# Linear attention and a highway layer: PSUM shared in four slots, weights cast by 128-row blocks, and a new order list

## The chip, the core and the metric

The kernel runs on one core of a Trainium2 chip. Its engines are TensorE (PE; PEld is its weight loading), VectorE (DVE), ScalarE (ACT), GpSimd (POOL) and SyncE (SP, which here only issues DMAs). PE writes its results to PSUM, eight banks of 128 x 512 fp32; DVE and ACT read and write PSUM, POOL does not in this kernel. The metric is the time of one execution on the device in microseconds, median over runs.

## What is computed

For 8 batches, 8 heads, 576 rows and head size 64, all fp32:

```python
q_s = softmax(q, axis=-1);  k_s = softmax(k, axis=2)      # over features; over rows
kv  = einsum('bhsd,bhse->bhde', k_s, v)                   # 64 x 64 per head
x   = einsum('bhsd,bhde->bhse', q_s, kv)  -> [4608, 512]
H = max(x @ w_h, 0);  T = sigmoid(x @ w_t + b_t)
out = T * H + (1 - T) * x
```

With th = tanh(z / 2) the gate is (1 + th) / 2. The kernel halves w_h - I on casting it, so that d = max(x(w_h - I)/2, -x/2) and out = (1 + th) * d + x.

## The kernel before

The 4608 rows are 36 tiles of 128. Batches go in pairs: tiles 9p to 9p+3 belong to the first, 9p+4 to 9p+7 to the second, 9p+8 to both. A step is named by its kind, a tile or batch, and a part; a suffix names its engine (A, D, P) or a variant.

Per batch: `k_`, `v_`, `q_` are loads on SP's queue (landing buffers for three batches); `ek` and `eq` are exponentials on ACT (`:F` for all of a batch in one); `vc` casts v to fp16 (POOL, unless A or D); `kv` is 72 small matmuls into a pair of banks, with the sums of k in an extra column; `kr`, `kn` (DVE) normalise it to fp16. `qt` transposes exp(q) on PE, `qc` copies that to SBUF.

Per tile: `xu` (PE, a pair of banks), `rs` and `x` (DVE) give normalised x; `xt` transposes it on PE and `xe` copies it to SBUF (ACT, or DVE with D); `mh` and `mt` are four 512-column matmuls each against w_h and w_t. `bw` seeds `mt`'s bank with the bias: a copy of `ball` on ACT or DVE, or, without a suffix, a matmul on PE. `th` is the tanh, `dd` gives d, `uu` gives (1 + th) * d on DVE from PSUM, or with `:P` in two instructions on POOL (L578, L579); `oo` adds x on POOL, `st` stores. Tiles 0, 4 and 5 (`HALVED`) go in two halves of heads, and the last tile, 35, in two halves of columns. `fill_n` are n matmuls of zeros.

`ORDER` (L16) is a list written out by a search; the program issues the steps in its sequence, so it fixes the sequence on each engine and on SP's queue, while across engines only data and buffers make one wait. An engine never passes a waiting step, and SP never passes a waiting DMA.

PSUM before: `ps_t` gives two banks in turn to the `mt` results, `ps_g` two to the `mh` results and the halved `xu`. The other four banks are two slots (`space`, L183), each either one pair or two singles; `kv`, `xu`, `qt` and `xt` use them. A transpose with `:W` takes one bank and 128-row matmuls; without it, it takes a pair and twice as many matmuls of 64 rows. A seed by ACT or DVE is added to by matmuls with `start=False`.

Weights before: each of four landed pieces of w_h and w_t (two 128-row blocks, 128 x 1024) is cast in one instruction, `whc` (L275) and `wtc` (L264); `whd` subtracts the identity first, block by block, on POOL.

## Time and profile before

| what | us |
|---|---|
| median of 3 runs | 119.06 |
| lowest and highest | 118.78, 119.47 |
| the profiled execution's own time | 118.52 |
| its span, first to last instruction | 116.7 |
| mean granted TensorE clock | 0.988 |

The profile shows one execution. Busy time is given per engine; a row of a timeline or of a group has start or count, duration, engine, source line, the operation, and the tiles written and read. Idle time before a row is put down to what ended it. The chain of waits is followed back from the last instruction. Loading takes 30.41 MB from HBM, storing 9.44 MB.

### The profile page before, as it was taken

How to read it: one execution, taken by the hardware profiler on the slowest of the kernel's cores; microseconds unless marked ns; L12 is line 12 of the kernel's file. 1: busy time of each engine (PE TensorE's matmuls, PEld its weight loads, DVE VectorE, ACT ScalarE, POOL GpSimd, SP SyncE). 2: the span in 40 equal slices, each digit the busy share in tenths (PEclk: the TensorE clock that was granted, in tenths of full speed). 3: DMA queues.
4: the chain of work that ended last, by engine and by line, in shares of the span. 5: the costliest groups of instructions: out<-in, count | busy, mean ns of one | idle time of the engine just before them, and what ended most of it. 6: DMA issues, size and time to landing. Idle time of an engine off the chain costs nothing.

```text
span 116.7 us, 3816 instructions
## 1 busy us (share of the span) xinstructions
PE 107.1 (92%) x1544; PEld 57.3 (49%) x1544; DVE 92.4 (79%) x216; ACT 90.7 (78%) x132; POOL 90.0 (77%) x104
## 2 busy tenths in 40 slices
...
GB/s 46 376 401 377 409 397 386 376 375 389 391 390 389 389 392 360 376 386 371 371 359 395 385 405 387 378 383 371 404 389 187 275 386 237 274 190 359 340 288 176
DMA packets 24198, 40.62 MB, mean 348 GB/s; under 512 B 5363, under 2 KB 11763, under 8 KB 24181
## 3 DMA queue, kind: packets, MB, share of 16 engines
...
q8 instruction: 12, 0.20, 0.7%
...
HBM read 30.41 MB, written 9.44 MB: 341 GB/s over the span
## 4 chain that ended last, share of the span: by engine, by line
PE 70%; DMA 14%; POOL 5%; issue 3%; DVE 2%; SPq 1%; ACT 1%; DVEq 0%; POOLq 0%
PE tps L539 25%; PE gps L547 24%; DMA w32t<-in_moe_w_t_dram 9%; DMA v<-in_v_dram 5%; PE pair L449 4%; PE one L504 4%; PE pair L316 4%; PE one L402 3%; POOL v L306 2%; PE pair L496 2%; PE pair L376 1%; POOL u L579 1%; POOL o L599 1%; DVE u L581 1%; PE pair L458 1%
## 5 line engine op out<-in xcount | busy, mean ns | idle before, releaser
L599 POOL TENSOR_TENSOR o<-u,x 128x512 f32<-128x512 f16 (+1 forms) x36 | 40.5, 1141 | 3.0 <-DVE u L581 2.0
L539 PE MATMUL tps<-w16t,xT 128*128 128x512 f16 (+1 forms) x144 | 36.6, 377 | 0.3 <-DVE tps L527 0.3
L547 PE MATMUL gps<-w16h,xT 128*128 128x512 f16 x144 | 36.8, 380 | 0.0
L567 DVE SCALAR_TENSOR_TENSOR d<-x,gps 128x512 f16<-128x512 f16 x36 | 24.2, 675 | 0.2 <-PE gps L547 0.2
L579 POOL TENSOR_TENSOR u<-g,d 128x512 f16<-128x512 f16 x19 | 21.9, 1155 | 2.7 <-DVE d L567 1.3
L306 POOL CAST v<-v 128x1152 f16<-128x1152 f32 (+1 forms) x13 | 12.3, 958 | 11.0 <-DMA v<-in_v_dram 11.0
L480 DVE TENSOR_TENSOR x<-pair,rs 128x512 f16<-128x512 f32 x27 | 18.2, 685 | 1.2 <-POOL o L599 0.2
L539 PEld LDWEIGHTS <-xT 128*128 128x128 f16 x148 | 12.9, 98 | 12.2 <-DVE xT L515 0.7
L300 ACT ACTIVATE ek<-k 128x576 f16<-128x576 f32 (+2 forms) x15 | 17.9, 1222 | 1.2 <-DMA k<-in_k_dram 1.2
L547 PEld LDWEIGHTS <-xT 128*128 128x128 f16 x144 | 12.5, 98 | 11.9 <-ACT xT L515 0.3
L525 ACT COPY tps<-ball 128x512 f32<-128x512 f32 x22 | 13.1, 594 | 3.8 <-DVE u L581 3.6
L561 ACT ACTIVATE th<-tps 128x512 f16<-128x512 f32 x19 | 11.3, 593 | 2.6 <-PE tps L539 2.5
L214 PE MATMUL one<-blank 128*128 128x512 f16 x40 | 11.4, 429 | 1.5 <-POOL blank L145 1.3
L578 POOL TENSOR_SCALAR g<-th 128x512 f16<-128x512 f16 x19 | 11.7, 617 | 0.7 <-ACT th L561 0.7
L581 DVE SCALAR_TENSOR_TENSOR u<-tps,d 128x512 f16<-128x512 f32 (+1 forms) x17 | 11.4, 670 | 1.0 <-ACT tps L563 0.5
L358 ACT ACTIVATE qe<-q 128x1024 f16<-128x1024 f32 (+3 forms) x9 | 9.2, 1052 | 3.3 <-DMA q<-in_q_dram 3.3
L563 ACT ACTIVATE tps<-tps 128x512 f32<-128x512 f32 (+1 forms) x17 | 9.8, 575 | 1.8 <-PE tps L539 1.8
L504 PE MATMUL one<-idh,x 128*128 128x128 f16 x100 | 9.5, 219 | 1.4 <-DVE xT L515 1.0
L504 PEld LDWEIGHTS <-x 128*128 128x128 f16 x100 | 7.1, 98 | 6.2 <-DVE x L485 1.4
L515 ACT COPY xT<-one 128x512 f16<-128x512 f16 (+1 forms) x13 | 6.9, 532 | 2.3 <-PE one L504 1.6
L353 ACT ACTIVATE qe<-q 128x1024 f16<-128x1024 f32 (+1 forms) x7 | 8.0, 1175 | 0.0
L449 PEld LDWEIGHTS <-eq 64*128 64x128 f16 (+1 forms) x240 | 4.6, 97 | 6.4 <-issue 5.5
...
## 6 DMA issues: line engine op xcount, KB each, us to landing
k<-in_k_dram SPq DMA_DIRECT2D x6, 1152.0 KB, 12.4
v<-in_v_dram SPq DMA_DIRECT2D x6, 1152.0 KB, 12.4
...
q<-in_q_dram SPq DMA_DIRECT2D x2, 1152.0 KB, 13.0
...
```

The lines of the kernel that those rows point to most:

```text
L300: nc.scalar.activation(t[:, :, c:c + n].rearrange("p j c d -> p c j d"), T[f"k32{b}"][:, c:c + n].rearrange("p c (j d) -> p c j d", j=NJ), ...
L306: copy(v16[b % NV][:, c:c + n, :, 0:D], T[f"v32{b}"][:, c:c + n].rearrange("p c (j d) -> p c j d", j=NJ))
L480: nc.vector.tensor_mul(t.rearrange("p k (w h) e -> p w k h e", w=2), pairs(i)[:, :, :, 1:129].rearrange("p w k (h e) -> p w k h e", h=2), ...
L504: nc.tensor.matmul(t[:, n], T[f"x{i}"][:, n0 + n % 2:n0 + 2 * P:2], idh, is_transpose=True, start=True, stop=True, skip_group_check=True)
L525: nc.scalar.copy(t[:, cs], ball[:, cs])
L539: nc.tensor.matmul(T[gate(i, k)][:, cs], T[f"xT{i}"][:, n], w16["t"][:, n, cs], start=False, stop=(n == parts[-1] and not first), skip_gro ...
L547: nc.tensor.matmul(t, T[f"xT{i}"][:, n], w16["h"][:, n], start=(first and n == parts[0]), stop=(n == parts[-1] and not (first and len(part ...
L567: nc.vector.scalar_tensor_tensor(t, T[f"x{i}"], -0.5, T[f"gps{i}"], op0=ALU.mult, op1=ALU.max)
L578: nc.gpsimd.tensor_scalar(g, T[f"th{i}"], 1.0, 1.0, op0=ALU.add, op1=ALU.mult)
L579: nc.gpsimd.tensor_mul(t, g, T[f"d{i}"])
L581: nc.vector.scalar_tensor_tensor(t[:, cs], T[gate(i, h)][:, cs], 1.0, T[f"d{i}"][:, cs], op0=ALU.add, op1=ALU.mult)
L599: eng.tensor_add(t[:, cs], T[f"u{i}_{h}"][:, cs], T[f"x{i}"][:, cs])
```

## The change

All eight banks are now four slots of two banks, and every step that uses PSUM asks for space in them. `bank_users` names the user of each step and what it wants: a pair, a single, a single written over its whole width by matmuls (full), or a single that ACT or DVE seeds, which must have been full or seeded before. `grant` walks the list once, when the program is built, and gives each user banks whose last user stands earlier in the list; a slot changes its form when both its banks are free. Pairs prefer slots 2 and 3 (banks 4 to 7). Weights are cast in eight instructions of 128 x 512, `whb` and `wtb`, one per 128-row block. The list is searched anew: loads, stores, engines and tile order differ from the 41st step on. By count: fills 40 matmuls to 33; `bw` on PE 6 to 5, on ACT 22 to 24, on DVE 9 to 8; `uu` on POOL 19 to 20; `xe` on DVE 19 to 27; `qc` on ACT 7 to 9; `vc` on POOL 13 to 11, on DVE 1 to 4; `qt` with `:W` 9 to 7.

```diff
 ORDER = """
 b_0 q_0_0 v_0_1 setupdve k_0_0 b_32 eq_0_0 bsplit setuppool fill_5 fill_8 bp v_0_0 bc qt_0_0 ek_0_1 v_0_3 ek_0_0 k_0_2
 v_0_2 vc_0_3:A bw_1 vc_0_0 ek_0_2 vc_0_2 q_0_4 vc_0_1:D ek_0_3 bw_0 w_h_0 fill_8 qc_0_0 whd_1:P kv_0_0 eq_0_1 w_h_2
-w_t_2 kr_0_0 whd_0:P whd_2:P setuplate w_t_0 k_1_2 v_1_2 q_1_0 k_1_0 v_1_0 fill_5 q_1_4 kn_0_0 q_2_0 k_2_0 eq_0_2
-xu_0_0 v_2_0 q_3_0 rs_0_0 whc_0:A x_0_0 k_3_0 fill_4 v_3_0 kv_0_1 fill_3 kr_0_1 kn_0_1 xu_0_1 rs_0_1 xu_1_0 rs_1_0
-qt_0_1 x_1_0 fill_6 whd_3:P qc_0_1 xt_1_0 xu_3_0 qt_0_2 qc_0_2:A xe_1_0:D fill_1 rs_3_0 x_3_0 x_0_1 xt_3_0 xu_2_0
-rs_2_0 whc_2:A x_2_0 xe_3_0 mh_1_0 mh_3_0 wtc_2 xt_2_0 dd_1 wtc_0:P mt_1_0 th_1_0 ek_1_2 xe_2_0:D xt_0_0 vc_1_3 xt_0_1
-ek_1_3 bw_3:D mh_2_0 mt_3_0 dd_2 xe_0_1:D xe_0_0 vc_1_2 eq_1_0 uu_1_0:P oo_1_0 th_3_0 ek_1_1 mt_0_1 kv_1_1 qt_1_0
-ek_1_0 dd_3 kr_1_1 kn_1_1 vc_1_0 mh_0_1 mh_0_0 mt_0_0 qc_1_0 xu_5_1 bw_2 rs_5_1 vc_1_1:A kv_1_0 th_0_0 bw_5:A mt_2_0
-eq_1_2 x_5_1 xt_5_1 dd_0 eq_1_1 qt_1_2 kr_1_0 kn_1_0 qc_1_2 xu_5_0 rs_5_0 x_5_0 xu_4_0 xe_5_1 xu_8_0 q_4_0 qt_1_1
-th_2_0 rs_8_0 xt_5_0 x_8_0 xe_5_0:D uu_3_0:P qc_1_1:A rs_4_0 mt_5_1 x_4_0 oo_3_0 mh_5_1 mt_5_0 bw_8:A xt_8_0 xe_8_0:D
-th_5_0 xu_6_0 xu_4_1 mh_5_0 uu_0_0:P oo_0_0 mt_8_0 uu_2_0:P eq_2_1 rs_6_0 x_6_0 xt_6_0 eq_2_0 th_8_0 rs_4_1 dd_5
-xu_7_0 mh_8_0 rs_7_0 uu_5_0:P qt_2_0 xe_6_0:D x_4_1 mh_6_0 x_7_0 ek_2_0:F xt_4_1 qc_2_0 qt_2_1 dd_8 qc_2_1 vc_2_2
-xe_4_1:D xt_4_0 bw_6 xe_4_0 mt_6_0 uu_8_0 bw_4:D qt_2_2 mh_4_0 vc_2_0:A xt_7_0 kv_2_0 oo_5_0 qc_2_2:A dd_6 mh_4_1
...
-qc_7_2:A xt_34_0 bw_30:A qc_6_2:A st_17_0 uu_31_0:P st_32_0 th_33_0 st_23_0 xu_35_0 st_14_1 dd_33 rs_35_0 uu_33_0
-xe_34_0 bw_34:A oo_33_0 x_35_0 dd_30 mt_30_0 st_16_1 th_30_0 uu_30_0 mh_34_0 xt_35_0:W mt_34_0 st_33_0 xe_35_0 oo_31_0
-th_34_0 mh_35_0 oo_30_0 bw_35_0 st_31_0 mt_35_0 st_30_0 bw_35_1 mt_35_1 th_35_0 dd_34 uu_34_0 oo_34_0 st_34_0 dd_35
-uu_35_0 oo_35_0 st_35_0 th_35_1 uu_35_1 oo_35_1:D st_35_1:A
+w_t_2 kr_0_0 whd_0:P whd_2:P w_t_0 kn_0_0 whb_0 fill_8 k_1_2 kv_0_1 k_1_0 whd_3:P kr_0_1 xu_0_0 kn_0_1 xu_0_1 qt_0_1
+wtb_3:P eq_0_2 rs_0_0 wtb_0:P x_0_0 q_1_4 whb_2 rs_0_1 fill_4 qc_0_1 x_0_1 xt_0_0 xe_0_0:D xt_0_1 xe_0_1:D v_1_2
+xu_3_0 v_1_0 rs_3_0 whb_3:D x_3_0 mh_0_1 xt_3_0 whb_1:D mh_0_0 dd_0 wtb_2 wtb_1:P q_1_0 mt_0_1 xu_1_0 q_2_0 setuplate
+rs_1_0 x_1_0 xe_3_0 qt_0_2 qc_0_2 ek_1_2 ek_1_3 mh_3_0 dd_3 bw_3 mt_3_0 xt_1_0 th_3_0 ek_1_1 v_2_0 xu_2_0 mt_0_0
+th_0_0 xe_1_0:D uu_0_0:P vc_1_3 vc_1_2 mh_1_0 eq_1_2 rs_2_0 x_2_0 xt_2_0 xe_2_0:D bw_6:D mt_1_0 eq_1_1 dd_1 uu_3_0
+bw_8:A bw_2:A mh_2_0 qt_1_1 vc_1_1 ek_1_0 qc_1_1:A dd_2 k_2_0 kv_1_1 vc_1_0:D kv_1_0 kr_1_1 qt_1_2 qc_1_2:A kn_1_1
+q_3_0 eq_1_0 th_1_0 mt_2_0 kr_1_0 th_2_0 kn_1_0 xu_6_0 qt_1_0 rs_6_0 x_6_0 eq_2_0 qc_1_0 xt_6_0 xe_6_0:D xu_8_0 rs_8_0
+xu_5_0 oo_0_0 eq_2_1 rs_5_0 x_8_0 mt_6_0 xu_5_1 xu_4_0 oo_3_0 xt_8_0 x_5_0 uu_1_0:P uu_2_0:P mh_6_0 k_3_0 rs_4_0
+rs_5_1 xu_4_1 th_6_0 xe_8_0:D xt_5_0 mt_8_0 vc_2_2 x_5_1 xt_5_1 qt_2_1 rs_4_1 xe_5_0:D x_4_1 xe_5_1:D x_4_0 dd_6
+th_8_0 mh_8_0 uu_6_0 mh_5_1 bw_5:A xt_4_0 qc_2_1:A vc_2_0 xt_4_1 xe_4_0:D xu_7_0 mt_5_0 v_3_0 bw_4:A rs_7_0 ek_2_0:F
+dd_8 oo_2_0 qt_2_0 mh_5_0 xe_4_1:D qc_2_0 x_7_0 mh_4_0 mt_5_1 dd_5 uu_8_0:P mh_4_1 oo_8_0 qt_2_2 qc_2_2 xt_7_0
+xe_7_0:D kv_2_0 bw_7:A kr_2_0 th_5_0 q_4_0 eq_3_0:F oo_6_0 kn_2_0 mt_7_0 th_7_0 dd_4 xu_11_0 rs_11_0 xu_10_0 rs_10_0
+x_10_0 x_11_0 mt_4_0 mh_7_0 uu_5_0:P xt_10_0:W xu_12_0 dd_7 xe_10_0 xt_11_0 xe_11_0:D bw_10:A mt_4_1 mh_10_0 th_4_0
+ek_3_2 rs_12_0 uu_7_0 oo_1_0 x_12_0 mt_10_0 uu_4_0 xt_12_0:W xe_12_0:D oo_5_0 ek_3_0 xu_9_0 rs_9_0 v_4_0 vc_3_0 qt_3_1
+x_9_0 mh_11_0 vc_3_2 qc_3_1 mh_12_0 xt_9_0:W th_10_0 dd_10 bw_12:A qt_3_0:W qt_3_2:W k_4_0 dd_11 kv_3_0 oo_4_0 qc_3_2
+mt_12_0 xe_9_0 q_5_0 qc_3_0:A kr_3_0 kn_3_0 dd_12 xu_17_0 bw_9:A bw_11:D xu_14_0 oo_7_0 eq_4_0:F uu_10_0:P rs_14_0
+x_14_0 th_12_0 oo_10_0 bw_14:A mh_9_0 mt_9_0 xt_14_0:W rs_17_0 uu_12_0:P mt_11_0 dd_9 xe_14_0:D mh_14_0 th_9_0 x_17_0
+uu_9_0 xu_13_0 qt_4_0 vc_4_2:A th_11_0 xt_17_0:W mt_14_0 rs_13_0 x_13_0 xu_16_0 qc_4_0:A xe_17_0:D bw_17:A dd_14
+xu_15_0 mh_17_0 mt_17_0 xt_13_0:W ek_4_0:F rs_15_0 oo_12_0 oo_9_0 rs_16_0 vc_4_0 x_15_0 th_17_0 uu_11_0:P dd_17
+th_14_0 xt_15_0:W oo_11_0 x_16_0 qt_4_1 bw_13:A kv_4_0 xe_13_0:D mh_13_0 xe_15_0:D v_5_0 uu_17_0 oo_17_0 bw_15:A
+kr_4_0 eq_5_0 qc_4_1 kn_4_0 xt_16_0:W vc_5_2:D q_4_9 xe_16_0:D mt_13_0 xu_20_0 xu_19_0 rs_19_0 v_6_0 rs_20_0 mt_15_0
+mh_15_0 dd_13 uu_14_0:P oo_14_0 mh_16_0 x_19_0 eq_5_1 xt_19_0 th_13_0 x_20_0 vc_5_0:A q_5_9 qt_5_1 dd_15 qc_5_1
+bw_16:A mt_16_0 xu_18_0 st_5_0 eq_5_2 k_5_0 th_15_0 uu_15_0 st_1_0 xe_19_0 qt_5_0 xt_20_0:W dd_16 mh_19_0 th_16_0
+xe_20_0:D bw_20:A mh_20_0 rs_18_0 x_18_0 dd_19 qc_5_0:A uu_13_0:P xu_21_0 xt_18_0 ek_5_0:F bw_19:D mt_20_0 mt_19_0
+qt_5_2:W st_1_1 eq_4_2 q_6_0 xe_18_0:D mh_18_0 th_19_0 st_3_1 oo_13_0 th_20_0 rs_21_0 x_21_0 bw_18:A qt_4_2:W dd_20
+st_14_1 uu_19_0 kv_5_0 dd_18 qc_4_2:A qc_5_2:A xt_21_0:W kr_5_0 kn_5_0 eq_6_1 mt_18_0 bw_21:A eq_6_0 xu_23_0 xe_21_0:D
+rs_23_0 xu_26_0 rs_26_0 mh_21_0 mt_21_0 uu_16_0:P oo_15_0 x_26_0 oo_16_0 x_23_0 th_18_0 xt_26_0:W xe_26_0 qt_6_0
+xt_23_0 dd_21 qt_6_1:W st_3_0 bw_23:D xe_23_0:D qc_6_0 st_14_0 mh_26_0 vc_6_0 xu_24_0 xu_22_0 uu_20_0:P oo_20_0
+th_21_0 bw_26:A mt_23_0 dd_26 st_5_1 oo_19_0 rs_24_0 vc_6_2:A rs_22_0 mh_23_0 x_24_0 x_22_0 mt_26_0 k_6_0 ek_6_0:F
+th_23_0 xt_24_0 kv_6_0 uu_18_0:P dd_23 qc_6_1 xe_24_0:D uu_23_0 th_26_0 kr_6_0 q_7_0 st_10_1 kn_6_0 v_7_0 xt_22_0:W
+uu_21_0:P mh_24_0 k_7_0 xe_22_0:D oo_21_0 oo_18_0 oo_23_0 xu_25_0 xu_28_0 rs_25_0 st_12_0 st_10_0 bw_24:A bw_22:A
+mt_24_0 mt_22_0 q_6_9 rs_28_0 x_25_0 xu_29_0 x_28_0 xt_25_0 dd_24 q_7_9 eq_7_0 qd_7_0 eq_7_1 qd_7_1 rs_29_0 xt_28_0:W
+th_24_0 mh_22_0 x_29_0 xe_25_0 th_22_0 xe_28_0:D xu_30_0 xt_29_0 uu_26_0:P rs_30_0 xe_29_0 oo_26_0 mh_28_0 mh_29_0
+dd_22 uu_22_0:P mh_25_0 st_19_0 uu_24_0:P bw_25:D dd_28 ek_7_0:F x_30_0 vc_7_2:A xu_27_0 bw_28:D rs_27_0 oo_22_0
+vc_7_0:D xt_30_0 mt_25_0 mt_28_0 xe_30_0 kv_7_0 dd_25 dd_29 th_25_0 oo_24_0 kr_7_0 mh_30_0 st_21_0 th_28_0 st_7_0
+uu_28_0 bw_30:A mt_30_0 st_17_0 uu_25_0:P x_27_0 xt_27_0 kn_7_0 xu_31_0 bw_29:A mt_29_0 st_12_1 bw_27:D xe_27_0:D
+mt_27_0 rs_31_0 x_31_0 xt_31_0 dd_30 bw_31:D eq_7_2 th_29_0 st_8_0 xu_34_0 rs_34_0 th_30_0 mh_27_0 st_16_0 xe_31_0
+oo_25_0 st_25_0 x_34_0 st_7_1 qt_7_2:W qc_7_2 mt_31_0 st_23_0 xt_34_0 dd_27 st_26_0 xu_33_0 eq_6_2 uu_29_0:P mh_31_0
+rs_33_0 th_27_0 bw_34:A xe_34_0:D qt_6_2:W qc_6_2:A th_31_0 mt_34_0 oo_29_0 x_33_0 xu_35_0 dd_31 oo_28_0 xu_32_0
+uu_27_0 rs_32_0 xt_33_0:W mh_34_0 uu_31_0 xe_33_0 bw_33:A th_34_0 x_32_0 mh_33_0 xt_32_0:W uu_30_0:P oo_30_0 st_30_0
+oo_31_0 st_31_0 dd_34 rs_35_0 uu_34_0 xe_32_0 mt_33_0 oo_34_0 oo_27_0 bw_32:A x_35_0 st_34_0 mh_32_0 th_33_0 xt_35_0:W
+xe_35_0 dd_33 uu_33_0 st_16_1 mt_32_0 th_32_0 st_28_0 oo_33_0 dd_32 uu_32_0 oo_32_0 st_33_0 mh_35_0 bw_35_0 bw_35_1
+mt_35_0 st_32_0 th_35_0 dd_35 mt_35_1 th_35_1 uu_35_0 oo_35_0 uu_35_1 st_35_0 oo_35_1:D st_35_1:A
...
     PS = bass.MemoryType.PSUM
-    ps_t = pool("ps_t", 2, space=PS)
-    ps_g = pool("ps_g", 2, space=PS)
...
+    def bank_users(step):
...
+        if kind in ("xu", "rs", "x"):
+            return [(f"xu{at[0]}_{at[1]}", "single" if at[0] in HALVED else "pair")]
+        if kind in ("kv", "kr", "kn"):
+            return [(f"kv{at[0]}", "pair")]
...
+        if kind == "bw" and at[0] < LAST:
+            return [(gate(at[0], 0), "seeded" if e else "full")]
...
+        if kind in ("mh", "dd"):
+            return [(f"gps{at[0]}", "full")]
...
+    place, held, shape, whole = {}, [None] * 8, ["single"] * 4, [False] * 8
+    SPARE = 0
+    def grant(user, want, now):
+        last = [-1 if h is None else final[h] for h in held]
+        free = [n < now for n in last]
+        idle = [free[2 * k] and free[2 * k + 1] for k in range(4)]
+        form = "pair" if want == "pair" else "single"
+        may = lambda k: shape[k] == form or (idle[k] and (k >= 2 or idle[k + 2]))
+        if want in ("pair", "early"):
+            k = min((k for k in (3, 2, 1, 0) if idle[k] and may(k)),
+                    key=lambda k: (want == "early" and k != 3, k < 2, max(last[2 * k:2 * k + 2])))
+            mine = [2 * k, 2 * k + 1]
+        else:
+            mine = [min((n for n in range(8) if free[n] and may(n // 2)), key=lambda n: (
+                want == "seeded" and not whole[n],
+                (3 if shape[n // 2] == "pair" else 2 if n >= 4 and free[n ^ 1] else 0) + (SPARE * (want == "single" and whole[n])),
+                last[n]))]
+            assert want != "seeded" or whole[mine[0]]
+        for n in mine:
+            held[n], whole[n] = user, want in ("seeded", "full")
+        shape[mine[0] // 2] = form
+        place[user] = (mine[0] // 2, form, mine[0] % 2)
...
     def space(user, n=None):
+        k, want, one = place[user]
+        if form[k] != want:
+            reopen(k, want)
+        return rooms[k][one if n is None else n]
...
+    def wt_cast(e, n):
+        src, dst = T[f"wt{n // 2 * 2}"][:, n % 2], w16["t"][:, n]
+        if e == "D":
+            nc.vector.tensor_scalar_mul(dst, src, 1.0)
+        else:
+            (nc.gpsimd.tensor_copy if e == "P" else nc.scalar.copy)(dst, src)
...
     def bw(e, i, h=0):
-        if i < LAST or h == 0:
-            t = T[gate(i, h)] = ps_t.tile([P, DM], FP32, tag="tps", name=f"tps_{i}_{h}")
-        else:
-            t = T[gate(i, h)] = space("last")[:, 0]
+        t = T[gate(i, h)] = space(gate(i, h))
...
     def mh(e, i, k):
-        t = once(f"gps{i}", lambda: ps_g.tile([P, DM], FP32, tag="gps", name=f"gps_{i}"))
+        t = once(f"gps{i}", lambda: space(f"gps{i}"))
```

120 lines of the change are left out of this document (44 added, 76 removed).

## The prediction

> **What bounds the kernel now.** I read the page first (busy time, then the chain of waits), then the windows, the chain in order of time, and last the timelines of the start and the end.
>
> ```profile
> span 116.7 us, 3816 instructions
> ...
> PE 107.1 (92%) x1544; PEld 57.3 (49%) x1544; DVE 92.4 (79%) x216; ACT 90.7 (78%) x132; POOL 90.0 (77%) x104
> ...
> GB/s 46 376 401 377 409 397 386 376 375 389 391 390 389 389 392 360 376 386 371 371 359 395 385 405 387 378 383 371 404 389 187 275 386 237 274 190 359 340 288 176
> ...
> PE 70%; DMA 14%; POOL 5%; issue 3%; DVE 2%; SPq 1%; ACT 1%; DVEq 0%; POOLq 0%
> ```
> ```profile
> 24.00:28.00 4.00, 3.39 (x65) 2.00 (x58) 2.91 (x9) 3.77 (x8) 3.66 (x5) 1.00 1.07 380
> ...
> 40.00:112.00 72.00, 71.46 (x1158) 37.75 (x1143) 64.27 (x138) 61.78 (x92) 66.27 (x66) 1.00 0.99 347
> ```
>
> The columns of a window are its length, then the busy time of PE, PEld, DVE, ACT and POOL, the granted clock, the DMA share and GB/s. From 40 to 112 us PE is busy in 71.46 of 72.00 us, and 70% of the chain is PE: this stretch ends when PE's work ends. POOL (66.27) and DVE (64.27) are close behind. The DMA engines are full too (share 0.99): 359 to 409 GB/s in slices 2 to 30 of 40, on average 385.
>
> The start is set by arrivals. Here an entry in brackets is the idle time before an instruction and what ended it.
>
> ```profile
> 7.88 10.72 DMA w32t<-in_moe_w_t_dram
> ...
> 39.80 0.81 PE pair L316 x67
> ...
> 64.89 0.39 issue
> ...
> 69.87 0.45 PE one L397 x8
> ...
> 82.46 0.62 PE pair L316 x71
> ...
> 88.24 0.37 PE pair L376 x16
> ...
> 102.37 0.86 PE gps L547 x4
> ```
> ```profile
> 17.78 1.89 PE L547 MATMUL gps<-w16h,xT 128*128 128x512 f16 x8
> ...
> 26.20 0.66 POOL L306 CAST v<-v 128x576 f16<-128x576 f32 x1 [0.18 <-DMA v<-in_v_dram]
> ...
> 37.41 1.14 POOL L306 CAST v<-v 128x1152 f16<-128x1152 f32 x1 [0.78 <-DMA v<-in_v_dram]
> ...
> 34.68 2.11 ACT L300 ACTIVATE ek<-k 128x2304 f16<-128x2304 f32 x1
> ...
> 37.68 0.27 PE L504 MATMUL one<-idh,x 128*128 128x128 f16 x2 [0.98 <-DVE xT L515]
> ```
>
> The last weight lands at 18.6, the last piece of v of batch 1 at 26.2, v of batch 2 at 37.4. PE waits for the last time at length (0.98) before 37.68; from `kv_2_0` at 39.80 to its last matmul it runs on, with 0.39 us of gap.
>
> ```profile
> 111.25 0.60 PE L539 MATMUL pair<-w16t,xT 128*128 128x256 f16 x4
> ...
> 38.51 3.38 POOL L599 TENSOR_TENSOR o<-u,x 128x512 f32<-128x512 f16 x3
> ...
> 107.91 5.28 POOL L599 TENSOR_TENSOR o<-u,x 128x512 f32<-128x512 f16 x5 [0.72 <-DVE u L581]
> ...
> 112.82 0.42 DVE L599 TENSOR_TENSOR o<-pair,x 128x256 f32<-128x256 f32 x1
> ```
>
> PE ends at 111.85, POOL at 113.19, DVE at 113.24; then the last stores. So POOL ends level with DVE's last add. The 38.51 row begins with `oo_5_0`, the first POOL step behind `kv_2_0` in the list; an add is 3.38 / 3 = 1.13.
>
> **The change part by part.** The prices used:
>
> ```profile
> L581 DVE SCALAR_TENSOR_TENSOR u<-tps,d 128x512 f16<-128x512 f32 (+1 forms) x17 | 11.4, 670 | 1.0 <-ACT tps L563 0.5
> L413 DVE COPY eq<-one 128x1024 f16<-128x1024 f16 x8 | 5.5, 688 | 0.7 <-PE one L402 0.3
> L515 DVE COPY xT<-one 128x512 f16<-128x512 f16 x12 | 4.9, 416 | 1.9 <-PE one L504 1.9
> L515 DVE COPY xT<-one 128x256 f16<-128x256 f16 x3 | 0.8, 281 | 0.0
> L515 ACT COPY xT<-one 128x512 f16<-128x512 f16 x10 | 5.8, 583 | 0.6 <-PE one L504 0.4
> L485 DVE TENSOR_TENSOR x<-pair,rs 128x512 f16<-128x512 f32 x6 | 4.1, 690 | 0.2
> L485 DVE TENSOR_TENSOR x<-xu,rs 128x256 f16<-128x256 f32 x6 | 2.5, 422 | 0.2
> L473 DVE RECIPROCAL rs<-pair 128x8 f32<-128x8 f32 x6 | 1.2, 204 | 0.6 <-PE pair L458 0.4
> L279 ACT ACTIVATE w16h<-w32h 128x1024 f16<-128x1024 f32 x2 | 2.1, 1058 | 0.9 <-POOL w32h L273 0.9
> L269 POOL CAST w16t<-w32t 128x1024 f16<-128x1024 f32 x1 | 1.0, 1037 | 2.4 <-DMA w32t<-in_moe_w_t_dram 2.4
> L306 DVE CAST v<-v 128x576 f16<-128x576 f32 x1 | 0.8, 754 | 0.0
> L283 DVE CAST b<-b 1x512 f16<-1x512 f32 x2 | 0.8, 384 | 1.3 <-DMA b<-in_moe_b_t_dram 1.3
> ACT tps L525 <- DVE u L581: 3.6, 6, 0.8
> 57.90 0.61 POOL L578 TENSOR_SCALAR g<-th 128x512 f16<-128x512 f16 x1
> 58.60 1.16 POOL L579 TENSOR_TENSOR u<-g,d 128x512 f16<-128x512 f16 x1
> 59.84 1.16 POOL L599 TENSOR_TENSOR o<-u,x 128x512 f32<-128x512 f16 x1
> k<-in_k_dram SPq DMA_DIRECT2D x6, 1152.0 KB, 12.4
> ```
>
> *Banks.* What the fixed rings of two cost is ACT's seed copies waiting for DVE's `uu` (3.6 us in total, 0.8 at most); PE has no row for a bank. Following `grant` down the new list, every pair goes to slots 2 and 3 (banks 4 to 7) and all but eleven single users after the start go to banks 0 to 3: much as before. I price the sharing itself at nothing; between -0.98 (PE's one long wait goes) and +0.8 (one such bank wait moves onto PE).
>
> *Weights.* Four casts of 128x1024 become eight of 128x512: ACT 3, POOL 3, DVE 2. ACT gains 3 x 0.5 us, POOL pays three halves of 1.04 for one whole (+0.5), DVE pays 2 x 0.384 to 2 x 0.754; I take 0.69 each, near the wide row, since all 128 partitions are cast. Behind `whb_0` on ACT waits `eq_0_2`; behind `whb_3` and `whb_1` on DVE wait `x_3_0` and `dd_0`. All of it is hidden: batch 0 is through PE before v of batch 1 (26.2) lets `kv_1_0` start. Without that cover the three POOL and DVE pieces would cost up to 1.5 us.
>
> *Fills and biases.* 40 fill matmuls become 33, seven of 0.216 (0.86 / 4), before 18 us where PE waits for arrivals: nothing on the path. One bias matmul less, also early.
>
> *Batch 1.* The loads of batch 1 arrive in another order; q_1_4 (640 KB) instead of q_1_0 (512) lies before `v_1_0`, so it lands 128 KB / 385 GB/s = 0.3 later, 26.5. Cast on DVE 0.75, `kv_1_0` 0.5, `kr` and `kn` 0.9, `xu_6_0` 0.3: 29.0. Then DVE, in order, up to `x_7_0`: full x 3 x 0.69, half x 4 x 0.42, sums 7 x 0.2, two eq copies 1.38, xe 2 x 0.42 and 4 x 0.28, dd and uu 3 x 0.67 = 10.5, so 39.5 by durations that overlap in the timeline by some 0.06 each (28 steps, so 38 to 39.5). PE's next gate is `kv_2_0`: k of batch 2 is now the third load, as v was before, lands at 37.4, and `ek_2_0` needs 2.11: 39.6. PE is idle more than before between 26 and 31 (about 2 us, `xu_6` waiting for `kn_1_0`), and saves the 0.98 before 37.68. I take `kv_2_0` at 39.6, 0.2 earlier than 39.80; bounds 39.3 (nothing later than k) and 41 (DVE's 10.5 with 1.5 of waits).
>
> *After kv_2.* The same work remains (tiles 9 to 35, parts of 4 and 7), less `mh_4_1` (two of 0.216), already done; three q transposes lose their :W and one gets it, 2 x (0.45 - 0.37) less. The blocks of 64-row matmuls between full ones number 27 in both lists. PE: -0.6. DVE gets 4 xe and 2 v casts (2 x 0.754 each) and loses two uu, two eq copies and a dd: about +1.5 on 64.3, in 71.4 us. ACT loses five xe. POOL loses an oo and three v casts (1.14 each) and gets two lifted uu (from 57.90 to 59.84: 1.94 with g).
>
> *POOL.* In the new list `vc_2_2` waits for v of batch 2, now the second load: 1,152 KB at 385 GB/s earlier than 37.4, so 34.3. Then two casts (1.14), `oo_2`, `uu_8`, `oo_8` (1.13 + 1.94 + 1.13): POOL begins the work behind `kv_2` at 40.8, where it began at 38.51. That work is 32 x 1.13 + 16 x 1.94 + 4 x 1.11 (casts back to back) = 71.6, before 33 x 1.13 + 14 x 1.94 + 7 x 1.11 = 72.2. So POOL's dense end is 112.4. At its end I follow `oo_34` behind `uu_34` (about 107.2), then `oo_27`, `oo_33`, `oo_32` behind `uu_32`, and half an add: 0.4 of waits, 112.8.
>
> *Loads and stores.* `st_14_1` now stands ahead of `k_6_0` on SP and waits for `oo_13_0`: POOL work of 12 x 1.13 + 6 x 1.94 + 3 x 1.11 = 28.5 behind 40.8, so 69.3. From the weights' 18.6 to the end of k_6 are 22,656 KB, 60.3 us at 385 GB/s: 78.9. `kv_6_0` comes near 83 (82.46 before), less 2.1 for `ek_6`: 80.9 is in time, by 2 us. I price it at nothing; what hides it is that margin.
>
> *End.* The last tanh, uu and oo follow PE's end as before (113.24 - 111.85 = 1.4). PE's end moves from 111.85 by 0.2 + 0.6 to 111.05, so DVE ends at 112.5, and POOL, at 112.8, is last.
>
> **Sum.** 113.24 becomes 112.8: -0.4. The profiled execution took 118.52 us (span 116.7 and 1.8 around it): 118.1. The median of the runs is 119.06, 0.54 above that execution, so 118.6.
>
> **The rivals.**
>
> (1) *More is gained.* If shared banks let work run ahead in the start, PE's 0.98 goes beyond the sum and POOL starts its stretch that much earlier: 117.6. Against it: PE is 99% busy after 40, and the start hangs on arrivals. The Trainium skill, Perfetto Trace Analysis, Matmul Optimizations, asks that all eight PSUM banks be used for parallelism, and so speaks for this rival; the trace gives it little to win, since its waits for a bank stand on ACT.
>
> (2) *POOL takes over (the other side).* The new list leaves POOL no slack: 71.6 us of work from 40.8, against PE's 71.4 from 39.6. Before, it had 74.7 us (38.51 to 113.19) for 72.2, so 2.5 us of waits and gaps were free. If they come again, POOL ends at 114.9, 1.7 later than 113.19, and the time is 120.7; with half of them, 119.5. It decides from about 1 us on. Against it: an engine that lags finds its inputs ready.
>
> (3) *DVE delays the start.* Between 29 and 39.5 DVE has 10.5 us of work in a row, and each x, xT and d that PE needs is in it. Waits above the overlap (28 x 0.06 = 1.5) delay `kv_2_0` and all after it; 2.5 us of waits make 119.6, 3.5 make 120.6. DVE's total goes from 92.4 to about 98 (eight xe, three v casts, two weight casts in; two eq copies, a uu, a seed out).
>
> (4) *k_6 comes late.* With 4% less than 385 GB/s, or `oo_13` six us late, `kv_6` waits 0.5 to 3 us: 119.1 to 121.6. A k load takes 12.4 us from issue to landing, so one held back is not made up.
>
> (5) *The clock falls.* PE between 26 and 31 would be some 60% busy, where now the window from 24 has 3.39 of 4.00.
>
> ```profile
> 110.00:116.70 6.70, 1.85 (x14) 1.13 (x12) 2.92 (x6) 1.25 (x3) 3.11 (x4) 0.79 0.65 250
> ```
>
> The only window below 1.00 is this one, with PE busy for 28%. Five to seven us at 0.79 would cost 1.1 to 1.5: 119.9. The Trainium skill, TensorE: Matmul & The Clock Gate, Part 1, says that an idle window of some 3.4 us halves the clock; by an estimate from that page one such window would cost 1.7 us. The trace agrees that a short gap (0.98) leaves the clock alone.
>
> **How the numbers follow.** A measurement of this kernel tells about 0.5% (0.6 us) from no change: faster is below 118.46, slower above 119.66. The forecast, 118.6 (its own range 117.9 to 119.5), has 0.46: 0.24 of it faster, 0.20 same, 0.02 slower, since its middle lies just inside the bound. (1) has 0.12, faster; (2) 0.15, of it 0.02 same; (3) 0.11, of it 0.02 same; (4) 0.11 and (5) 0.05, slower. Faster 0.36, same 0.24, slower 0.40. The range leaves out a third of (1) and the upper ends of (2) to (4), under 0.2 together: 117.4 to 121.0.
>
> **What would show it.** Right: the L316 block of `kv_2_0` at 39.3 to 40, PE over 99% busy from there, PE's last matmul near 111.1, the last oo on POOL near 112.8. The weights: the first L547 near 17 instead of 17.8, and no gain from it. Wrong: POOL without gaps but ending beyond 113.5 (2), a gap of PE before `kv_2_0` ended by DVE (3), ACT idle before an `ek` for DMA of k near 80 (4), a clock under 1.00 between 24 and 35 (5), PE's gap before 40 gone (1). The forecast fails most easily in the start, where I followed 28 DVE steps by hand, and in POOL's want of slack.

## The result: 0.4% slower

The median over 20 runs is 119.50 us (118.58 to 120.87) against 118.81 (118.53 to 119.47) for the kernel before in the same comparison: ratio 1.0040, 95% interval 1.0021 to 1.0059. The forecast was 118.6, with a range of 117.4 to 121.0. The range held the time, but the sign was wrong. The ratio leaves out executions in a slower state (after: the three at 120.43 to 120.87); medians and ranges keep them. The profiled execution took 119.21 us, 0.29 below its median.

The head of the page after, with the chain of waits by engine as its last line:

```profile
span 117.4 us, 3838 instructions
...
PE 105.9 (90%) x1552; PEld 56.4 (48%) x1552; DVE 95.5 (81%) x225; ACT 88.0 (75%) x127; POOL 91.4 (78%) x106
...
PE 67%; DMA 21%; DVE 5%; ACT 2%; SPq 1%; issue 1%; DVEq 0%; ACTq 0%
```

PE has 1.2 us less work than before (105.9 for 107.1) and a share of 67% of the chain instead of 70%; DMA has 21% of it instead of 14%. How long PE itself waits is read from windows.

To compare two executions they need a common zero. I take W, the moment at which POOL begins to cast the last weight that lands. From the timelines of POOL, first before, then after:

```profile
18.66 1.04 POOL L269 CAST w16t<-w32t 128x1024 f16<-128x1024 f32 x1 [2.37 <-DMA w32t<-in_moe_w_t_dram]
```
```profile
18.92 1.18 POOL L308 CAST w16t<-w32t 128x512 f16<-128x512 f32 x2 [0.63 <-DMA w32t<-in_moe_w_t_dram]
```

In both, the same loads lie ahead of this one, so I don't count the 0.26 us between them as the change's. (Two kernels below, g1 and g2, whose lists are the same to far behind this point, differ by 0.73 here.) The windows from W to `kv_2_0`, and from there to PE's last matmul, before:

```profile
18.66:39.73 21.07, 19.15 (x217) 11.08 (x215) 16.43 (x41) 17.61 (x27) 17.47 (x20) 1.00 1.06 385
39.73:111.85 72.12, 71.73 (x1168) 38.02 (x1166) 64.23 (x138) 62.00 (x91) 66.39 (x66) 1.00 0.99 347
```

and after (columns as in the prediction: length, then busy PE, PEld, DVE, ACT and POOL, clock, DMA share, GB/s):

```profile
18.92:41.05 22.13, 19.36 (x226) 11.12 (x222) 17.59 (x46) 16.48 (x23) 16.36 (x22) 1.00 1.06 386
41.05:112.65 71.60, 70.98 (x1180) 37.83 (x1180) 66.51 (x143) 61.36 (x89) 68.37 (x68) 1.00 1.00 341
```

Up to `kv_2_0` the change costs 1.06 us: 0.21 more PE work and 0.85 more idle (2.77 for 1.92). Behind it, it gains 0.52: 0.75 less work, against 0.23 more idle (0.62 for 0.39). That is +0.54; with 0.26 from W, and about 0.1 less behind PE's end, it makes the 0.69 between the two profiled executions (119.21 and 118.52). In one line: PE's work fell by 0.54, and its idle time rose by 1.08.

This account for every kernel that was run, in us. Idle is length less PE's busy time; work is PE's busy time from W to its last matmul. Each line up to "PE end" is one profiled execution. The ratio compares all executions of a kernel with those of the kernel before in the same comparison, where the median of before lay between 118.79 and 119.01. It is not the quotient of two medians, which for the change would be 1.0058.

| kernel | W | kv_2_0 − W | idle before it | idle behind it | work | PE end − W | median | ratio (95%) |
|---|---|---|---|---|---|---|---|---|
| before | 18.66 | 21.07 | 1.92 | 0.39 | 90.88 | 93.19 | 118.81 | |
| after | 18.92 | 22.13 | 2.77 | 0.62 | 90.34 | 93.73 | 119.50 | 1.0040 (1.0021–1.0059) |
| n_banks_alone | 19.10 | 21.18 | 2.45 | 6.14 | 92.50 | 101.09 | 126.87 | 1.0674 (1.0646–1.0703) |
| w1_weights_alone | 19.33 | 21.09 | 2.20 | 0.40 | 90.53 | 93.13 | 119.20 | 1.0030 (1.0014–1.0045) |
| u1_whole_weights | 19.14 | 22.05 | 2.41 | 1.11 | 90.44 | 93.96 | 119.26 | 1.0038 (1.0020–1.0056) |
| e1_kv11_early | 19.65 | 24.89 | 5.35 | 0.00 | 90.32 | 95.67 | 122.45 | 1.0292 (1.0256–1.0327) |
| s1_kn_act | 19.04 | 21.94 | 2.51 | 0.08 | 90.47 | 93.06 | 119.24 | 1.0019 (0.9994–1.0043) |
| e3_k6_first | 19.35 | 22.12 | 2.76 | 0.00 | 90.05 | 92.81 | 118.80 | 0.9992 (0.9970–1.0014) |
| s2_kn_k6 | 19.20 | 21.92 | 2.49 | 0.01 | 90.24 | 92.74 | 118.83 | 0.9999 (0.9979–1.0020) |
| g1_old_start | 18.92 | 21.19 | 2.15 | 1.22 | 90.63 | 94.00 | 119.72 | 1.0068 (1.0044–1.0093) |
| g2_old_start_k6 | 19.65 | 21.10 | 2.33 | 0.73 | 90.16 | 93.22 | 118.89 | 0.9993 (0.9978–1.0009) |
| b1_xe_early | 18.82 | 20.09 | 0.79 | 0.44 | 90.91 | 92.14 | 118.58 | 0.9971 (0.9951–0.9990) |
| b2_xe_o1 | 19.06 | 20.01 | 0.94 | 0.62 | 90.90 | 92.46 | 118.44 | 0.9971 (0.9947–0.9994) |
| g3_old_start_xe | 18.92 | 20.51 | 1.68 | 1.07 | 90.22 | 92.97 | 118.46 | 0.9965 (0.9953–0.9977) |
| t1_new_start | 18.98 | 23.71 | 2.93 | 0.01 | 91.56 | 94.50 | 118.91 | 1.0012 (0.9981–1.0043) |
| f1_fills | 19.75 | 22.13 | 2.75 | 0.82 | 90.40 | 93.97 | 120.05 | 1.0098 (1.0063–1.0134) |
| f2_start_fills | 19.12 | 23.24 | 2.46 | 0.53 | 91.63 | 94.62 | 119.12 | 1.0014 (0.9993–1.0034) |
| f3_k6_fills | 19.70 | 22.11 | 2.74 | 0.00 | 90.19 | 92.93 | 119.06 | 1.0016 (1.0000–1.0032) |

The profiled executions of t1 and f2 ran with a lowered clock for some microseconds, so their columns up to "PE end" are not those of their medians.

Where the idle time comes from is read from the timelines after. PE around batch 1, at `kv_2_0`, and at the one gap behind it:

```profile
26.57 0.48 PE L355 MATMUL pair<-v,ek 64*64 64x65 f16 x36 [0.81 <-POOL v L345]
27.55 0.48 PE L355 MATMUL pair<-v,ek 64*64 64x65 f16 x36 [0.49 <-DVE v L345]
29.75 0.39 PE L496 MATMUL pair<-kvb,eq 128*128 128x130 f16 x4 [0.64 <-DVE kvb L377]
31.18 0.40 PE L542 MATMUL one<-idh,x 128*128 128x128 f16 x4 [0.58 <-DVE x L523]
41.05 0.80 PE L355 MATMUL pair<-v,ek 64*64 64x65 f16 x72
...
95.54 0.77 PE L355 MATMUL pair<-v,ek 64*64 64x65 f16 x72 [0.61 <-ACT xT L550]
```

DVE between `kv_1_0` and `xu_6_0`:

```profile
28.09 0.17 DVE L367 RECIPROCAL rz<-pair 128x2 f32<-128x2 f32 x1 [0.59 <-PE pair L355]
28.29 0.59 DVE L377 TENSOR_TENSOR kvb<-pair,rz 64x128 f16<-64x128 f32 x2
28.90 0.17 DVE L367 RECIPROCAL rz<-pair 128x2 f32<-128x2 f32 x1
29.11 0.59 DVE L377 TENSOR_TENSOR kvb<-pair,rz 64x128 f16<-64x128 f32 x2
```

And ACT's two late exponentials of k, of batch 6 and of batch 7:

```profile
81.56 2.12 ACT L339 ACTIVATE ek<-k 128x2304 f16<-128x2304 f32 x1
...
91.84 2.12 ACT L339 ACTIVATE ek<-k 128x2304 f16<-128x2304 f32 x1 [1.16 <-DMA k<-in_k_dram]
```

PE waits four times for batch 1 (26.57 to 31.18, 2.52 together); from 31.18 to `kv_2_0` it has no gap to speak of. The gap before 95.54 is `kv_7_0`: the k of batch 7 came 1.16 us too late for ACT. The profile names ACT's xT copy, which stood behind that `ek` in ACT's queue.

### The profile page after: what moved, and what is told of

Its sections match the earlier page's. It is cut to its first block, busy times and chain, and to the rows that moved or that the text cites. A ratio compares the mean times of both kernels' runs of the same rounds, so it can differ in the third digit from the quotient of the medians.

```text
span 117.4 us, 3838 instructions
## 1 busy us (share of the span) xinstructions
PE 105.9 (90%) x1552; PEld 56.4 (48%) x1552; DVE 95.5 (81%) x225; ACT 88.0 (75%) x127; POOL 91.4 (78%) x106
## 4 chain that ended last, share of the span: by engine, by line
PE 67%; DMA 21%; DVE 5%; ACT 2%; SPq 1%; issue 1%; DVEq 0%; ACTq 0%
PE one L582 24%; PE one L574 23%; DMA v<-in_v_dram 11%; DMA q<-in_q_dram 10%; PE pair L487 5%; PE one L542 5%; PE pair L355 4%; PE one L441 2%; PE pair L534 2%; PE pair L415 1%; SPq L269 1%; DVE kvb L377 1%; PE pair L496 1%; DVE u L616 1%; ACT v L345 1%; DVE v L345 1%
## 5 line engine op out<-in xcount | busy, mean ns | idle before, releaser
L574 PE MATMUL one<-w16t,xT 128*128 128x512 f16 (+1 forms) x148 | 36.9, 374 | 0.0
L582 PE MATMUL one<-w16h,xT 128*128 128x512 f16 x144 | 36.5, 380 | 0.2 <-ACT w16h L319 0.2
L602 DVE SCALAR_TENSOR_TENSOR d<-x,one 128x512 f16<-128x512 f16 x36 | 24.0, 672 | 0.8 <-PE one L582 0.8
L345 POOL CAST v<-v 128x1152 f16<-128x1152 f32 (+1 forms) x11 | 10.0, 930 | 9.0 <-DMA v<-in_v_dram 8.9
L560 ACT COPY one<-ball 128x512 f32<-128x512 f32 x24 | 13.9, 590 | 2.9 <-DVE d L602 1.5
L596 ACT ACTIVATE th<-one 128x512 f16<-128x512 f32 x20 | 11.6, 591 | 4.1 <-PE one L574 2.2
L616 DVE SCALAR_TENSOR_TENSOR u<-one,d 128x512 f16<-128x512 f32 (+1 forms) x16 | 10.6, 662 | 0.8 <-ACT one L598 0.4
L598 ACT ACTIVATE one<-one 128x512 f32<-128x512 f32 (+1 forms) x17 | 9.4, 556 | 1.3 <-PE one L574 1.2
L553 DVE COPY xT<-one 128x512 f16<-128x512 f16 (+1 forms) x21 | 7.9, 380 | 2.5 <-PE one L542 2.4
L355 PE MATMUL pair<-v,ek 64*64 64x65 f16 x576 | 6.6, 193 | 2.0 <-POOL v L345 0.8
```

The lines of the kernel that those rows point to most:

```text
L345: copy(v16[b % NV][:, c:c + n, :, 0:D], T[f"v32{b}"][:, c:c + n].rearrange("p c (j d) -> p c j d", j=NJ))
L560: nc.scalar.copy(t[:, cs], ball[:, cs])
L574: nc.tensor.matmul(T[gate(i, k)][:, cs], T[f"xT{i}"][:, n], w16["t"][:, n, cs], start=False, stop=(n == parts[-1] and not first), skip_gro ...
L582: nc.tensor.matmul(t, T[f"xT{i}"][:, n], w16["h"][:, n], start=(first and n == parts[0]), stop=(n == parts[-1] and not (first and len(part ...
L602: nc.vector.scalar_tensor_tensor(t, T[f"x{i}"], -0.5, T[f"gps{i}"], op0=ALU.mult, op1=ALU.max)
L616: nc.vector.scalar_tensor_tensor(t[:, cs], T[gate(i, h)][:, cs], 1.0, T[f"d{i}"][:, cs], op0=ALU.add, op1=ALU.mult)
```

## The experiments

Two theories were tested. By the first, the loss is the start (batch 1 comes through PE later). By the second, it is the load of k_6 held behind a store. Rivals were the shared banks, the split weights and the fewer fills.

**The banks alone.** The old list with old casts, under the new allocator. So that every user finds banks, four steps are named earlier, and `xu_35_0` with its two steps on DVE stands later.

```diff
-... bw_20:A uu_18_0 ... xu_35_0 ... rs_35_0 ... x_35_0 ... mt_30_0
+... uu_18_0 bw_20:A ... mt_30_0 xu_35_0 rs_35_0 x_35_0
 ... (dd_12, th_14_0 and dd_13 are named earlier too)
```

> The old list and the old weight casts with the new sharing of all eight banks. Four steps (dd_12, th_14_0, dd_13, uu_18_0) are named a few places earlier in the list so that a written bank is free for each seed copy, their order on their engines unchanged, and xu_35_0 with its two DVE steps stands behind mt_30_0, since the sharing has no free slot for it before. Theory A (sharing costs nothing by itself): kv_2_0 at 39.7 to 40.0, PE's last matmul at 111.8 to 112.3 (up to 0.4 from the moved xu_35_0), the time 118.7 to 119.2. Rival E (sharing itself makes waits): gaps of PE in front of matmuls of a bank that another user has just left, the time 119.5 or more. Rival F (sharing lets work run ahead): 118.2 or less.

It took 1.0674 of the time. The start is untouched (21.18 behind W); behind `kv_2_0` PE is idle for 6.14 us instead of 0.39, and its work there takes 73.77 us instead of 71.73. Two rows of its PE timeline, and the waits of ACT (total, times, longest):

```profile
52.16 0.27 PE L440 MATMUL one<-idh,qe 128*128 128x128 f16 x2 [1.28 <-ACT eq L451]
75.69 0.27 PE L440 MATMUL one<-idh,qe 128*128 128x128 f16 x2 [0.91 <-DVE u L615]
```
```profile
ACT one L559 <- DVE d L601: 6.5, 5, 2.3
```

A transpose of q needs no `u`: it waits for the bank that `u` reads. Six rows of this kind, between 45.75 and 83.72, make 4.0 of the 6.14 us. So sharing is not free by itself; the order decides. In the list of the change no such row stands on PE behind `kv_2_0`, and ACT's seeds wait 2.6 us for a bank that DVE reads, 3.6 before:

```profile
ACT one L560 <- DVE d L602: 1.5, 3, 1.0
...
ACT one L560 <- DVE u L616: 1.1, 2, 0.7
```

The Trainium skill, Perfetto Trace Analysis, Matmul Optimizations, asks that all eight banks be used. Both kernels do; which step may use which bank in which order was worth 6.7% here, and no rule on the number of banks tells that.

**The weights alone, and the change without them.** w1 is the old kernel with its four casts split; u1 the new one with four whole casts, none on DVE.

```diff
-whc_0:A ... whc_2:A ... wtc_2 ... wtc_0:P
+whb_0 whb_1 ... whb_2 whb_3 ... wtb_2 wtb_3 ... wtb_0:P wtb_1:P
```

> The kernel before with its weight casts alone split into 128-row blocks, in place and on the same engines (six on ACT, two on POOL). Theory A (the weights are hidden): mh of tile 1 may start up to 0.5 us earlier, kv_2_0 stays at 39.7 to 40.2, the time within 0.2% of the kernel before (118.7 to 119.2). Rival H (the extra instructions on ACT delay the ek and th steps of batch 1): kv_2_0 0.2 to 0.6 later, 119.2 to 119.6.

> The changed kernel with its weight casts undone alone: whole pieces of 256 rows on ACT and POOL at the first place of the new casts, none on DVE. Theory A (the weights are hidden by the arrival of batch 1): the first mh of the list 0.3 to 1.2 us later than 16.51, PE's work of batch 0 later by as much and its idle time between 25 and 31 smaller by as much, kv_2_0 the same to 0.2, the time 119.3 to 119.6. Rival H (the blocks bring the start forward after all): kv_2_0 and the end 0.5 to 1.0 later, 120.0 to 120.5. Rival J (the blocks cost): 119.0 or less.

u1 takes the time of the change (1.0038 for 1.0040), though its first `mh` comes 0.8 us later (17.32 for 16.51). w1 traces like the kernel before (93.13 for 93.19), yet its time is 0.3% above it: its runs have the spans of before, and the difference lies around the span (2.1 us for 1.8). No run says why; the change itself has 1.8. The first of the two pieces on DVE was cheaper than I took:

```profile
16.49 0.39 DVE L317 TENSOR_SCALAR w16h<-w32h 128x512 f16<-128x512 f32 x1
```

**Batch 1 earlier.** e1 (from the change) moves the casts and `kv` of batch 1 forward.

```diff
-... uu_0_0:P vc_1_3 vc_1_2 ... bw_8:A bw_2:A mh_2_0 qt_1_1 ... vc_1_0:D kv_1_0 kr_1_1 ... kn_1_1
+... vc_1_3 vc_1_2 uu_0_0:P ... bw_2:A mh_2_0 kv_1_1 qt_1_1 ... kr_1_1 kn_1_1 k_2_0 vc_1_0:D kv_1_0 ...
```

> The changed kernel with four edits in the start: vc_1_3 and vc_1_2 ahead of uu_0_0 on POOL (they stood behind its 3.09 us wait for th_0_0), kv_1_1 ahead of qt_1_1 on PE, kr_1_1 and kn_1_1 ahead of vc_1_0 on DVE, and bw_8 on ACT later so that a slot is free for kv of batch 1. Theory A (the chain v_1_0, cast, kv_1_0, four normalising steps, xu_6 delays the start and all behind it): kv_1_1 runs near 24.9 instead of 26.57, kn_1_0 ends at 28.9 instead of 29.71, xu_6 starts at 29.0 instead of 29.75, kv_2_0 at 40.2 to 40.5 instead of 41.05, PE's end 0.5 to 0.8 earlier, the time 118.7 to 119.0 (0.4% to 0.7% under the changed kernel). Rival B (POOL's own work sets the end): kv_2_0 moves as in A, POOL still ends at 113.7 to 114.0, the time stays at 119.3 to 119.5. Rival C (the queue of DVE and ACT steps between 30 and 41, not the chain, sets kv_2_0): xu_6 moves, kv_2_0 stays at 40.9 to 41.1, the time 119.4.

It lost 2.9%. From its timelines of POOL, DVE and PE:

```profile
25.98 1.27 POOL L345 CAST v<-v 128x576 f16<-128x576 f32 x2 [5.02 <-DMA v<-in_v_dram]
29.11 0.69 DVE L602 SCALAR_TENSOR_TENSOR d<-x,one 128x512 f16<-128x512 f16 x1 [2.90 <-POOL u L614]
31.34 0.48 PE L355 MATMUL pair<-v,ek 64*64 64x65 f16 x36 [3.00 <-DVE v L345]
44.54 0.80 PE L355 MATMUL pair<-v,ek 64*64 64x65 f16 x72
```

POOL waits 5 us for v_1_2, and what was put behind the cast waits with it: `uu_0_0`, then `dd_2` on DVE, then the v cast behind that, then `kv_1_0`. As a repair it missed, but it prices a late start. PE is idle for 2.6 us more before `kv_2_0` (5.35 for 2.77); 0.62 comes back, because the wait for k_7 is gone (0.00 for 0.62 behind `kv_2_0`), and PE's end is 1.94 later behind W. The medians differ by more, 2.95 us. Four of the six executions had mean clocks of 0.971 to 0.982, the other two, at 121.85 and 121.93, 0.991 and 0.993; so a part of the 2.95 may be the clock's, and no run separates it. Most of a late start is paid, not all of it.

s1 moves only `kr_1_1` and `kn_1_1`, and the cast of `vc_1_0` to ACT.

```diff
-... qc_1_1:A dd_2 k_2_0 kv_1_1 vc_1_0:D kv_1_0 kr_1_1 qt_1_2 qc_1_2:A kn_1_1
+... vc_1_0:A qc_1_1:A dd_2 k_2_0 kv_1_1 kr_1_1 kn_1_1 kv_1_0 qt_1_2 qc_1_2:A
```

> The changed kernel with the start's chain alone shortened: the cast vc_1_0 on ACT ahead of qc_1_1 instead of on DVE, and kr_1_1 and kn_1_1 named right behind kv_1_1, so that DVE does them while v_1_0 is being cast. Nothing else moves. Theory A (PE is without a break from xu_6 to kv_2_0 and on to its end, so each us that xu_6 comes earlier is kept to the end): kn_1_1 ends at 27.9 instead of 28.9, kn_1_0 at 29.2 instead of 29.7, xu_6 0.5 earlier, kv_2_0 at 40.5 instead of 41.05, both counted from the same arrival of the weights (18.92 in the changed kernel's profile), the time 118.9 to 119.1 (0.4% under the changed kernel, 0.0% to 0.2% above the kernel before). Rival C (eq_1_0 and the ACT queue behind it set what follows): xu_6 moves and kv_2_0 doesn't, 119.4. A loss is possible if qc_1_1, now 0.7 later on ACT, becomes what xu_6 waits for.

`kv_1_0` then waited for `kn_1_1`:

```profile
28.18 0.48 PE L355 MATMUL pair<-v,ek 64*64 64x65 f16 x36 [1.00 <-DVE kvb L377]
```

since both halves of a `kv` use one pair of banks, and `kv_2_0` came only 0.19 earlier behind W. The time, 1.0019, lies between the change and no change; its interval reaches both.

**k_6 first.** In e3 the load of k_6 stands ahead of the store it waited behind.

```diff
-... st_14_1 uu_19_0 ... mt_26_0 k_6_0 ek_6_0:F
+... k_6_0 st_14_1 uu_19_0 ... mt_26_0 ek_6_0:F
```

> The changed kernel with one step moved on SP: the load k_6_0 ahead of the store st_14_1, so that it no longer waits with the five stores at 65.17 (8.14 us). Theory A: k_6 issues at 64 to 65 instead of 73.41, the loads behind it have 1,152 KB less ahead of them, ek_7 loses its 1.16 us wait for k_7, the 0.61 us gap of PE before kv_7 at 95.54 is gone, PE ends 0.4 to 0.6 earlier, the time 118.9 to 119.1. Rival B (POOL sets the end): the gap goes, POOL still ends at 113.9 to 114.0, the time stays at 119.4 to 119.5. Rival D: the gap stays, because the cast vc_7_2 on ACT stands in front of kv_7 by itself: 119.4.

SP's queue after (start, length of the issue, count):

```profile
65.17 8.14 SPq L654 DMA_DIRECT2D out_dram<-o  x5
73.41 0.54 SPq L269 DMA_DIRECT2D k<-in_k_dram  x1
...
78.03 1.19 SPq L269 DMA_DIRECT2D k<-in_k_dram  x1
```

and the loads' effect, windows after:

```profile
74.00:76.00 2.00, 2.00 (x84) 1.30 (x82) 1.90 (x5) 1.97 (x5) 2.00 (x3) 1.00 0.90 259
76.00:78.00 2.00, 2.00 (x32) 0.99 (x31) 1.56 (x5) 2.00 (x4) 1.84 (x3) 1.00 0.94 316
```

e3's issue of k_6, its exponential of batch 7, the same windows and the window from `kv_2_0` on:

```profile
66.97 0.53 SPq L269 DMA_DIRECT2D k<-in_k_dram  x1
```
```profile
90.89 2.13 ACT L339 ACTIVATE ek<-k 128x2304 f16<-128x2304 f32 x1
```
```profile
74.00:76.00 2.00, 2.00 (x84) 1.39 (x82) 1.92 (x5) 1.97 (x6) 2.00 (x3) 1.00 1.05 404
76.00:78.00 2.00, 2.00 (x32) 0.90 (x31) 1.52 (x5) 2.00 (x4) 1.92 (x3) 1.00 1.02 401
41.47:112.16 70.69, 70.69 (x1180) 37.57 (x1180) 66.60 (x143) 61.45 (x89) 68.16 (x68) 1.00 0.98 343
```

In the change SP waits in the 8.14 us of store issues, the DMA engines run short of work (259 and 316 GB/s for 404 and 401), and that loss is passed down the queue to k_7, though k_6 itself is in time (`ek_6` at 81.56 has no wait). With k_6 first, `ek_7` and `kv_7_0` do not wait, PE has no idle time left behind `kv_2_0`, and the stretch is 0.91 shorter. Of that, 0.62 is the idle time; 0.29 is shorter work of the same 1180 matmuls, which vary by as much between the traces of this list (70.69 to 71.04). The time is that of the kernel before: the loss is gone, and the forecast gain has not come. POOL's end moves with PE's, by the same 0.92 behind W: here POOL follows, it does not set the end.

s2 is s1 with k_6 first.

> The edits of the run before (vc_1_0 on ACT, kr_1_1 and kn_1_1 earlier) and k_6_0 ahead of st_14_1 on SP together. Theory A: both gains add up, 0.5 in the start and 0.6 to 0.9 behind kv_2_0, no gap of PE in front of kv_7, the time 118.2 to 118.5, which is 0.4% to 0.6% under the kernel before. Rival B (POOL becomes the end once PE is 1.4 us earlier): POOL ends as late as with k_6_0 alone (94.15 us behind the arrival of the last weight) and the time stays at 118.7 to 118.9.

It gives 0.9999: k_6 again, and nothing to see from `kn_1_1`.

**The old start under the new list.** g1 takes the old list up to `kv_2_0` (casts split where they stand) and the new one behind it; g2 is g1 with k_6 first.

```diff
-new list: b_0 ... kv_2_0 ... st_35_0
+old list: b_0 ... kv_2_0, then what is left of the new list, in its order
```

> The changed kernel (shared banks, weights cast in 128-row blocks) with the old list up to kv_2_0, the casts split in place, and the new list from there on (th_6, dd_6, mh_4_1, xe_7, oo_2, oo_8 and uu_6 then follow kv_2_0, since the old list has not done them by then). Theory A: kv_2_0 at 39.7 to 40.0, then 71.6 of PE plus 0.2 for the moved mh_4_1, less 0.4 if k_7 is not late: PE's last matmul at 111.3 to 111.8, the time 118.2 to 118.8. Rival B (POOL): POOL has 71.6 + 2 x 1.13 + 1.94 us of work behind 38.5, so it ends at 114.5 or later and the time is 119.5 to 120. Rival G (the new list behind kv_2_0 is itself slower): kv_2_0 at 39.8 and PE's last matmul still at 112.3 or later.

> The old start under the shared banks with the new list behind kv_2_0, and k_6_0 ahead of st_14_1. Theory A (the new list behind kv_2_0 is the faster one, once k_7 is in time; the new start is the slower one): the 1.04 us of PE's gaps between 80 and 90 go, PE ends 71.7 to 72.0 behind kv_2_0 instead of 72.8, the time 118.6 to 118.9. Rival B (POOL, which is 5.9 us behind at v_3 and ends level with DVE, is the bound): POOL's end stays at 114.2 and the time at 119.6.

The old start gives back 0.94 us up to `kv_2_0` (21.19 for 22.13), and the rest then takes 1.21 more: 0.60 more idle and 0.61 more work, 0.32 of it work that the new start had already done. Undoing the start alone thus doesn't bring the time back. Again k_6 alone brings either one level with before (0.9993 and, in e3, 0.9992).

**Idle time before kv_2_0 taken away.** b1 is the old kernel with one DVE copy moved ahead of two steps, aimed at the 0.98 us that PE waited for it.

```diff
-xt_4_1 qc_2_0 qt_2_1 dd_8 qc_2_1 vc_2_2 xe_4_1:D
+xt_4_1 qc_2_0 xe_4_1:D qt_2_1 dd_8 qc_2_1 vc_2_2
```

> The kernel before with one step moved on DVE: xe_4_1 ahead of dd_8 and qc_2_1. There PE waits 0.98 us for it before xt_4_0, its only long wait in the start. Theory A (PE is without a break from there to its end, so every us of its idle time before kv_2_0 is a us of the time): the 0.98 goes, kv_2_0 comes 0.8 to 1.0 earlier (20.1 to 20.3 us behind the arrival of the last weight instead of 21.07; the cast vc_2_2 on POOL, which ended at 38.55, allows 38.6), PE's end 0.8 to 1.0 earlier, the time 118.0 to 118.2 (0.7% to 0.8% under the kernel before). Rival B (POOL, which ended level with DVE at 113.2, is a second bound): the time falls by 0.3 or less. Rival I (the next thing, k or v of batch 2, is late at once): kv_2_0 moves by less than 0.3.

```profile
18.82:38.91 20.09, 19.30 (x219) 10.99 (x217) 15.85 (x40) 17.84 (x28) 16.86 (x19) 1.00 1.06 385
```

`kv_2_0` comes 0.98 earlier behind W, PE ends 1.05 earlier, but the time is only 0.3% lower (0.34 us by the ratio). In this trace POOL's last add ends 94.62 behind W, 0.09 later than before, and POOL waits for free output buffers:

```profile
109.06 3.37 POOL L599 TENSOR_TENSOR o<-u,x 128x512 f32<-128x512 f16 x3 [0.64 <-DMA out_dram<-o]
112.77 0.67 POOL L599 TENSOR_TENSOR o<-u,x 128x256 f32<-128x256 f16 x1 [0.33 <-DMA out_dram<-o]
```

b2 gives those tiles five buffers instead of three.

```diff
-op.tile([P, DM], FP32, tag="o1", bufs=3, name=f"o32_{i}")
+op.tile([P, DM], FP32, tag="o1", bufs=5, name=f"o32_{i}")
```

> The kernel before with xe_4_1 ahead of dd_8 and qc_2_1, as in the run of that alone (0.9971 of the time before), and five buffers instead of three for the output tiles that are stored singly. Theory A (PE's gain of 1.05 was lost to oo steps on POOL that waited 0.64 and 0.33 for a store to free their buffer): those waits go, POOL and DVE end 0.6 to 0.9 earlier, the time 117.9 to 118.2 (0.993 of the time before). Rival B (POOL's own work is the bound): no waits for stores are left, but POOL ends within 0.3 of where it did and the time stays at 118.5.

The waits are gone, and the ends of PE and of POOL are both 0.73 earlier behind W than in the kernel before, yet the ratio stays 0.9971 (0.73 us would be 0.994). So more buffers did not bring the rest of the gain; where it goes stays open. g3 moves the same copy in g2:

> The old start under the shared banks with the new list behind kv_2_0, k_6_0 ahead of st_14_1, and xe_4_1 ahead of dd_8 and qc_2_1 as well. Theory A: 0.8 to 1.0 under the run without that last move (118.89), so 117.9 to 118.1. Rival B (POOL sets the end): POOL ends where it did, 94.5 us behind the arrival of the last weight, and the time stays at 118.7 to 118.9.

It gave 0.9965, the best of all, and faster than both kernels; b1, b2 and g3 can't be told from one another.

**Start and fills.** t1 (from the change, k_6 first) loads v_1_2 ahead of q_1_4, gives `d` a fourth buffer and moves a dozen steps of the start; f1 puts five fill matmuls back into the change; f3 is f1 with k_6 first, f2 is t1 with the fills. The cut is of f1.

```diff
-... xu_0_0 kn_0_1 xu_0_1 qt_0_1 ...
+... xu_0_0 kn_0_1 fill_3 xu_0_1 fill_2 qt_0_1 ...
```

> The changed kernel with k_6_0 ahead of st_14_1 and its start rearranged so that PE waits less for batch 1: the load v_1_2 ahead of q_1_4, its casts ahead of uu_0_0 on POOL (with a fourth buffer for d, which uu_0_0 then frees later), vc_1_0 on ACT, kr_1_1 and kn_1_1 right behind kv_1_1, ek_1_0 ahead of the q steps, qc_1_1 on DVE, eq_1_0 ahead of qc_1_2. Theory A (PE's idle time before kv_2_0 is what the new start costs): kn_1_0 ends 0.7 to 1.0 earlier than 29.70, PE's idle time between the weights and kv_2_0 falls from 2.77 to about 2.0, kv_2_0 comes 0.6 to 0.9 earlier than 22.13 us behind the last weight, the time 118.0 to 118.3 (with k_6_0 alone 118.8). Rival C (the DVE and ACT queues behind xu_6 set kv_2_0): xu_6 moves, kv_2_0 stays at 21.9 to 22.1, the time 118.7 to 118.9. A loss is possible where q_1_4, now 0.7 later, holds up qt_1_1.

> The changed kernel with five fill matmuls put back, three ahead of xu_0_1 and two ahead of qt_0_1, where PE waits 0.69 and 0.50 us. Theory K (without them the clock falls between 14 and 18 us in some executions, and so lengthens them): PE is busy for 1.6 or more of the 2.00 us from 12, no execution has a mean clock under 0.985, the highest times (120.1 to 120.9) go, the median falls from 119.5 to 119.2 to 119.4, while the lowest stays near 118.6. Rival L (fills are worth nothing): median 119.4 to 119.6 with the same spread. They could cost up to 0.2 if they delay xu_0_1 or qt_0_1.

> The changed kernel with k_6_0 ahead of st_14_1 and the five fills. Theory K: as with k_6_0 alone (118.8) but without its highest times (120.0 and 120.7), median 118.6 to 118.8, highest under 119.4. Rival L: median 118.8 and the same spread.

> The rearranged start with k_6_0 earlier, and the five fills. Theory A and K: clock at 1.00 from 10 to 20 us, PE's idle time between the weights and kv_2_0 at 2.3 or less (2.77 in the changed kernel), kv_2_0 0.2 to 0.7 earlier than 22.13 us behind the last weight, the median 118.4 to 118.6, highest under 119.2. Rival C (other queues set kv_2_0): kv_2_0 at 22.0 to 22.2, median 118.7 to 118.9.

None gained: t1 1.0012, f2 1.0014 and f3 1.0016 are not better than e3's 0.9992, and f1 (1.0098) is worse than the change. Why is not shown: in its trace PE's end is 0.24 later behind W, and W itself 0.83 later. t1's twelve times fall into two groups, seven at 118.38 to 118.97 with mean clocks of 0.990 to 0.998, and five at 120.04 to 120.49 with 0.964 to 0.983; the seven have a median of 118.68, against 118.79 before, so even they show no clear gain. The fills keep PE busy where the change left it idle (12 to 14 us: 0.82 of 2.00; with them 1.96), but that bought no time in the medians. The new start's own idle time therefore was never removed on the chip. That idle time before `kv_2_0` costs time rests on e1 (added, and for the most part paid) and b1 (taken away from the old start, and about a third returned).

## Why the prediction was wrong

**The sum.** It had PE's end 0.8 earlier and the end of the kernel 0.4 earlier. Behind W, PE's end came 0.54 later, and with W 0.80. Without W's 0.26 it missed the forecast 111.05 by 1.34 us: 1.19 of that arose before `kv_2_0`, 0.15 behind it. The work behind `kv_2_0` was right (−0.6 forecast, −0.75 measured); the waits were not, in two steps. The base of the sum was high as well: the median of before, 119.06 from three runs, is 118.81 over 20, so that −0.4 meant 118.4.

**Batch 1** failed, as the larger part. Forecast for `kv_2_0`: 39.6, bounds 39.3 to 41; it came at 41.05 (40.8 without W's 0.26). Its first steps hold: `v_1_0` cast at 26.7 and `kv_1_0` at 27.55, as summed. Then "kr and kn 0.9": the rows at 28.09 to 29.70 show 1.62, since both halves are normalised there. `kr_1_1` is named behind `kv_1_0`, and its row at 28.09 waited 0.59 for the pair that `kv_1_0` wrote until 28.03, though its own half, `kv_1_1`, had ended at 27.05. That made `xu_6_0` 29.75 instead of 28.7. The 10.5 us of DVE's steps behind it were right (30.2 to 40.6, of which 1.1 idle). But I took the arrival of k as PE's next gate and never summed PE's own queue between `xu_6_0` and `kv_2_0`: from 31.18 it runs without a gap until 41.05. `ek_2_0`, which I had at 37.4, started at 38.88 in ACT's order and ended at 41.00, level with PE, held by a seed that waited for DVE:

```profile
38.35 0.59 ACT L560 COPY one<-ball 128x512 f32<-128x512 f32 x1 [0.46 <-DVE u L616]
38.88 2.12 ACT L339 ACTIVATE ek<-k 128x2304 f16<-128x2304 f32 x1
```

**Loads and stores**, priced at nothing behind a margin of 2 us, failed, and this alone decides between a loss and none (e3: 1.0040 to 0.9992). k_6 was late at SP (73.41, where I had some 69.3): `oo_13_0` ended at 70.76, and three more stores, which I had not counted, stand between `st_14_1` and k_6. It was still in time for `ek_6`, as argued; the price appeared one load later, at k_7: 1.16 us of ACT, 0.61 of PE. I had priced the held load, not the queue behind it.

**Banks** at nothing: right for this list (PE has no such wait, ACT's shrank from 3.6 to 2.6), and wrong as a general statement (n_banks_alone: 8 us). **Weights**: hidden, as said (u1); their pieces on DVE cost about 0.4 each, not 0.69. **Fills**: nothing on the path; putting them back gained nothing. **POOL**: dense end, and no bound:

```profile
39.33 1.16 POOL L614 TENSOR_TENSOR u<-g,d 128x512 f16<-128x512 f16 x1 [0.88 <-DVE d L602]
...
106.52 7.47 POOL L634 TENSOR_TENSOR o<-u,x 128x512 f32<-128x512 f16 x7
```

It ends at 113.99, DVE at 114.03; its stretch began about 41.7 instead of 40.8, since `uu_8_0` had waited 0.88 for `dd_8` on DVE. **End**: 114.03 − 112.65 = 1.38 behind PE's end, as forecast (1.4).

**The rivals.** (1), more gained: not here, though b1 shows that the 0.98 it spoke of can be had. (2), POOL: no (e3). (3), a later start: its size came true (119.6 forecast with 2.5 us of waits, 119.5 measured), but by luck, since the wait for k_7 is part of it; nor did its mechanism, since PE's queue and the normalising of batch 1 made the start late, not waits between DVE's steps. (4), k_6 late: half right, as k_7. (5), the clock: 1.00 throughout the start in the change's profile, but not in every execution: three of the 20 have mean clocks of 0.962 to 0.981 and took 119.60 to 120.87 us, while none of 119 executions of the kernel before, in the later comparisons, lies under 0.988. The mean of the other 17 is still 0.4% above that of before.
